# One-bank PSUM tiles for the layers that follow an attention, in place of its two-bank tiles

## The chip, the cores and the metric

One core of one Trainium2 chip. The metric is the device time of one execution in microseconds (us), as the median of several runs.

## The reference, cut to what matters

An attention with 16 heads (2 batches of 8, 768 positions, 64 wide), masked to keys of the query's hash bucket, feeds two dense layers over 1536 tokens of width 512:

```python
q_bits = (np.einsum('bhsd,dk->bhsk', q, proj) > 0)      # k_bits in the same way
mask = q_bucket[:, :, :, None] == k_bucket[:, :, None, :]
scores = np.where(mask, scale * np.matmul(q, k.transpose(0, 1, 3, 2)), -1000000000.0)
attn = softmax(scores); x = np.matmul(attn, v)          # to rows of 512
h = x @ w_in;  x = (h - np.tanh(h)) @ w_out             # first layer, 2048 wide
g = x @ w_gate; silu = g * (1.0 / (1.0 + np.exp(-g)))
return (silu * (x @ w_val)) @ w_out2                    # second layer, 1536 wide
```

## The kernel before, in words

**Order.** Nothing is looped on the chip. Every step is declared once to `Plan.op` (a step is a group of instructions on one engine) with the keys that it reads and writes, an estimated duration and a due time. `Plan.order` plays these through and gives one fixed order for all engines; the loops at the end of `lsh_attention_moe_kernel` write the instructions out in it. Keys name single PSUM banks: `("s", z, 0)`, `("s", z, 1)`, `("t", 0)`, `("t", 1)`, `("x", 0)`, `("h", 0)`. The waits on the chip are not written in the kernel: the framework puts them in, from what each instruction reads and writes of a tile.

**Attention.** A step of 128 queries makes its scores (L653) in one of two `s` tiles of two banks, one bank for each half of the 768 keys. VectorE takes the maximum over both banks (L662), ScalarE the exponentials (L664); TensorE transposes the result into the two banks of the one `t` tile (L682), and a copy empties it (L688). The product with the values goes to `x` (L706). All eight banks are taken: two `s` tiles of two banks, a `t` tile of two, `x` and `h` of one each.

**Layers.** The layers start while the attention ends. A unit is 256 columns of `w_in`, `w_gate` or `w_val` for one half of the tokens. By a scheme of the Strassen kind it takes seven products, each of six matmuls of 128x384 (L850). Products 0, 3, 5 and 6 add up in the first bank of one `s` tile, products 1 and 4 in the second bank of that tile, and product 2 takes a bank of a ring of four (`t` 0, `t` 1, `x`, `h`). Units take the two `s` tiles in turn. Between products ScalarE copies a bank out (`snap`, L830) and VectorE adds such a copy (`add`, L833). A finished block gets tanh (L791) or the sigmoid (L798), a subtraction or product on VectorE or GpSimd (L779), and is split in a high part (ScalarE, L784) and a low part (L779), into `op`. The block of product 4 stays in its bank for all of this. Here the steps read the second bank while products 5 and 6 write the first:

```python
PRODUCTS = (
    ("A11", "B11", 0, True), ("S1", "T1", 2, True), ("A12", "B21", 1, True), ("S2", "T2", 0, False),
    ("S4", "B22", 2, False), ("S3", "T3", 0, False), ("A22", "T4", 0, False),
)
banks = [s_t[z][:, 0, 0:TB], None, s_t[z][:, 1, 0:TB]]
RING = [(("t", 0), t_t[0][:, 0, :]), (("t", 1), t_t[0][:, 1, :]), (("x", 0), x_t[0]), (("h", 0), h_t[0])]
```

An output group is six matmuls (L904; 384 columns in layer 1, 512 in layer 2) into a bank of the same ring, emptied by L914, L915, L917, L928 or L933, and in part added up in memory by a DMA on GpSimd's queue (L941, L950). The order mixes products with output groups.

**Weights.** They come as 64-bit floats in 68 chunks, loaded into two `raw` buffers by SyncE (L271). VectorE makes each into 32-bit numbers (L273, L276, L279), then they are combined and split (L285, L287, L305, L307, L322, L324). A load waits until VectorE has done with the chunk two before it.

Of the kernel before, what the change touches and what calls it, by code (L numbers as in the profile page):

```python
# [21 lines left out]
TB = 384  # L22
NTK = NB * S
NSB = NTK // S
DM = 512
# [39 lines left out]
class Plan:  # L65
# [9 lines left out]
    def __init__(self):  # L75
        self.ops = []
        self.writers, self.readers = {}, {}
        self.n_first = 0

    def op(self, eng, fn, r=(), w=(), due=0.0, lat=None, late=False, after=0.0, alt=None, port=()):  # L80
        n = len(self.ops)
        deps = set()
        for k in r:
            deps.update(self.writers.get(k, ()))
        for k in w:
            deps.update(self.writers.get(k, ()))
            deps.update(self.readers.get(k, ()))
        for k in r:
            self.readers.setdefault(k, []).append(n)
        for k in w:  # L90
            if k in r:
                self.writers.setdefault(k, []).append(n)
            else:
                self.writers[k] = [n]
                self.readers[k] = []
        deps.discard(n)
        eng = {e: t * (1 if e == "PE" or not self.n_first else self.SAFE) for e, t in eng.items()}
        self.ops.append((eng, fn, deps, due, self.LAT if lat is None else lat, late, after,
                         DUE["alt"] if alt is None else alt, port))
# [86 lines left out]
def lsh_attention_moe_kernel(ctx: ExitStack, tc: tile.TileContext, qT, kT, vP, proj, cst, wts, out):  # L186
# [41 lines left out]
    ones_b = csb[:, 128:129]  # L228
    bias_b = csb[:, 129:130]
    pj = const.tile([128, 32], F32, name="pj")  # L230
    s_t = tiles(ctx, "s", 2, [128, 2, 512], space=PSUM)
    t_t = tiles(ctx, "t", 1, [128, 2, 512], space=PSUM)
    x_t = tiles(ctx, "x", 1, [128, 512], space=PSUM)
    h_t = tiles(ctx, "h", 1, [128, 512], space=PSUM)
    late = {}

    counts = {}

# [537 lines left out]
    EARLY, XDUE, EALT, ZDUE = 14, 13, 1.0, (-4, 4)  # L776

    def tt(dst, dk, a, ak, b, bk, alu, due, port):
        op({"DVE": dve(TB), "POOL": pool(TB)} if port else {"DVE": 0.56}, lambda e: e.tensor_tensor(out=dst, in0=a, in1=b, op=alu),  # L779
           r=[ak, bk], w=dk, due=due, alt=ALT, port=BOTH * port)  # L780

    def split_g(key, src, sk, due, psum):
        (hi, hk, h1), (lo, lk, l1) = g_slot(), g_slot()
        op({"ACT": 0.52}, lambda g: g.activation(out=hi, in_=src, func=ACTF.Copy), r=[sk], w=[hk] + h1, due=due)  # L784
        tt(lo, [lk] + l1, src, sk, hi.bitcast(F32), hk, ALU.subtract, due + 0.6, not psum)
        gh[key] = hi, lo, [hk, lk]


    def block_tanh(key, src, sk, due, psum, keep, spare=None):
        t, tk, t1 = spare or t_slot(1)  # L790
        op({"ACT": 0.51}, lambda e: e.activation(out=t, in_=src, func=ACTF.Tanh), r=[sk], w=[tk] + t1, due=due)  # L791
        d, dk = (src, sk) if keep else (t, tk)
        tt(d, [dk], src, sk, t, tk, ALU.subtract, due + 0.6, not psum)
        split_g(key, d, dk, due + 1.2, keep and psum)

    def block_silu(key, src, sk, due, psum, keep, spare=None):
        t, tk, t1 = t_slot(2)
        op({"ACT": 0.51}, lambda e: e.activation(out=t, in_=src, func=ACTF.Sigmoid), r=[sk], w=[tk] + t1, due=due)  # L798
        tt(t, [tk], src, sk, t, tk, ALU.mult, due + 0.6, not psum)
        sg[key] = t, tk  # L800

# [8 lines left out]
        ("S4", "B22", 2, False), ("S3", "T3", 0, False), ("A22", "T4", 0, False),  # L810
    )

    RING = [(("t", 0), t_t[0][:, 0, :]), (("t", 1), t_t[0][:, 1, :]), (("x", 0), x_t[0]), (("h", 0), h_t[0])]

    def bank_slot():
        return RING[ring("bank", len(RING))[1]]

    def products(name, i, sb):
        layer = 1 if name == "in" else 2
        after = due_at(nst - (EARLY if i < 2 else 14)) if layer == 1 else 0.0  # L820
        wk = need((name, i), clock[0], after)
        w = wi_t[wk[1]]
        z = sets[0] = 1 - sets[0]
        bkeys = [("s", z, 0), None, ("s", z, 1)]
        banks = [s_t[z][:, 0, 0:TB], None, s_t[z][:, 1, 0:TB]]
        (c0, k0, f0), (c1, k1, f1), (c2, k2, f2) = c_slot(), c_slot(), c_slot()
        block = {"in": block_tanh, "gate": block_silu, "val": block_val}[name]

        def snap(dst, dk, bank, bk, due):
            op({"ACT": 0.49}, lambda e: e.activation(out=dst, in_=bank, func=ACTF.Copy), r=[bk], w=dk, due=due)  # L830

        def add(dst, dk, bank, bk, c, ck, due):
            op({"DVE": 0.56}, lambda e: e.tensor_tensor(out=dst, in0=bank, in1=c, op=ALU.add), r=[bk, ck], w=[dk], due=due)  # L833

        def product(n):
            xn, wn, bi, first = PRODUCTS[n]
            if bi == 1:
                bkeys[1], b = bank_slot()
                banks[1] = b[:, 0:TB]
            bank, bk = banks[bi], bkeys[bi]  # L840
            d = clock[0]
            clock[0] += 6 * MM3
            wi = WN[wn]
            wp = wk + ("aaabbcc"[wi],)

            def mm(e):
                m = 0
                for k in range(2):
                    for wpart, xpart in terms:
                        e.matmul(  # L850
                            out=bank, lhsT=w[:, wpart, wi * 256 + k * 128:wi * 256 + k * 128 + 128],
                            rhs=x_at(sb, xn, xpart, k), start=first and m == 0, stop=m == 5, skip_group_check=True,
                        )
                        m += 1

            op({"PE": 6 * MM3}, mm, r=[wp + (0,), wp + (1,)] + [("X", sb, xn, h, k) for h in range(2) for k in range(2)]
               + [bk] * (not first), w=[bk], due=d, lat=0.25)
            e = clock[0]
            if n == 0:
                snap(c0, [k0] + f0, bank, bk, e)  # L860
            elif n == 1:
                snap(c1, [k1] + f1, bank, bk, e)
            elif n == 2:
                add(bank, bk, bank, bk, c0, k0, e)
                block((layer, i, sb, 0, 0), bank, bk, e + 0.6, True, True, (c0, k0, []))
            elif n == 3:
                snap(c2, [k2] + f2, bank, bk, e - 1)
            elif n == 4:
                add(bank, bk, bank, bk, c2, k2, e)
                block((layer, i, sb, 0, 1), bank, bk, e + 0.6, True, True, (c2, k2, []))  # L870
            elif n == 5:
                add(c1, k1, bank, bk, c1, k1, e - 1)
                block((layer, i, sb, 1, 1), c1, k1, e + 1, False, False)
            else:
                block((layer, i, sb, 1, 0), bank, bk, e, True, False)

        return product
# [4 lines left out]
    def out_group(layer, i, sb, j):  # L882
# [6 lines left out]
        t, m = divmod(j, n)  # L889
        size = (TB, DM)[layer - 1]  # L890
        gs = [gh[layer, i, sb, t, f] for f in range(2)]
        k, ps = bank_slot()
        ps = ps[:, 0:size]

        def mm(e):
            c = 0
            for f in range(2):
                w = wo_t[wks[f][1]]
                for wpart, gpart in terms:
                    if layer == 1:  # L900
                        lhs, rhs = w[:, wpart, m * 128:m * 128 + 128], gs[f][gpart]
                    else:
                        lhs, rhs = gs[f][gpart][:, m * 128:m * 128 + 128], w[:, wpart, :]
                    e.matmul(out=ps, lhsT=lhs, rhs=rhs, start=c == 0, stop=c == 5)  # L904
                    c += 1

        op({"PE": dur}, mm, r=[wk + (h,) for wk in wks for h in range(2)] + [g for gg in gs for g in gg[2]], w=[k],
# [3 lines left out]
        if layer == 1 and i in (0, NP1 - 1):  # L911
            if i == 0:
                op({"DVE": dve(TB), "ACT": 0.5}, lambda g:
                   g.activation(out=acc_at(sb, j), in_=ps, func=ACTF.Copy) if g is nc.scalar else  # L914
                   g.tensor_copy(acc_at(sb, j), ps), r=[k], w=[("acc", sb, j)], due=e, late=True)  # L915
            else:
                op({"DVE": 0.57}, lambda g: g.tensor_tensor(  # L917
                    out=acc_at(sb, j), in0=ps, in1=acc_at(sb, j), op=ALU.add,
                ), r=[k, ("acc", sb, j)], w=[("acc", sb, j)], due=e, late=True)
        elif layer == 2 and i == NP2 - 1:  # L920
            if m == 0:
# [3 lines left out]
                op({"SP": 0.5}, lambda g, at_=parts[0][0]: g.dma_start(out=at_(3).rearrange("p (j c) -> p j c", j=3), in_=o),  # L925
                   r=[("o", sb, t)], w=[key for _, key, _ in parts] + [k for _, _, f in parts for k in f], due=e - 25, lat=4.0)
            at_, key = stages["last"][m]
            op({"DVE": dve(DM)}, lambda g: g.tensor_tensor(out=at_(), in0=ps, in1=at_(), op=ALU.add), r=[k, key], w=[key], due=e)  # L928
            op({"SP": 0.5}, lambda g: g.dma_start(out=out[sb * S + j * 128:sb * S + j * 128 + 128, :], in_=at_()), r=[key], w=[], due=e)
        else:  # L930
            at_, key, first = stage(layer, m)
            op({"ACT": 0.18 + size / 1200, "DVE": dve(size)}, lambda g, at_=at_:
               g.activation(out=at_(), in_=ps, func=ACTF.Copy) if g is nc.scalar else g.tensor_copy(at_(), ps),  # L933
               r=[k], w=[key] + first, due=e, late=layer == 2, alt=EALT)
            if m == 0:
                stages[layer, "at"] = at_
# [74 lines left out]
        out_group(*outs.pop(0))  # L1011

    order, first_late = plan.order()
    with tc.manual_schedule():
        for n, e, _ in order[:first_late]:
            plan.ops[n][1](eng[e])
        at.close()
        with ExitStack() as mo:
            late["x1"] = tiles(mo, "x1", 1, [128, NG * TB], F32R)[0]
# [61 lines left out]
```

## Time and profile before

| | |
|---|---|
| median of 3 runs | 803.41 us (802.49 to 804.92) |
| the profiled execution | 803.86 us, span 802.1 us |
| TensorE matmuls, weight loads | 766.6 us, 661.5 us busy |
| VectorE, ScalarE, GpSimd | 589.4, 466.8, 359.7 us busy |
| granted clock of TensorE | 1.0 over the whole span |
| chain that ended last | TensorE 76%, VectorE 11%, DMA 4%, ScalarE 3% of the span |

PE is TensorE's matmuls and PEld its weight loads, DVE VectorE, ACT ScalarE, POOL GpSimd, SP SyncE. A group of instructions is named by line, engine, operation and tiles, as `PE L850 MATMUL s<-x,wi`: buffer numbers are left out, so that `s` is any bank of either `s` tile. Idle time is put down to what released the waiting instruction. Six matmuls of 384 columns start over 1.04 us when nothing waits, and a matmul's row reaches past its weight load's, so a short wait shows in the weight loads first.

### The profile page before, as it was taken

The numbers are of one execution on the slowest core, as the hardware profiler recorded it, in microseconds if no ns is written. First come the engines' busy times: TensorE is split into PE (matmuls) and PEld (weight loads), VectorE is DVE, ScalarE is ACT, GpSimd is POOL, SyncE is SP. The second block draws the span as 40 slices with busy tenths as digits, with TensorE's granted clock in tenths as the row PEclk, the third lists the DMA queues.
The fourth block names the chain that finished last, engine by engine and source line by source line (L and its number), as shares of the span: only waits on it lengthen the run. The fifth ranks groups of instructions, "written<-read, shape, count | busy, mean of one in ns | idle before, by whom it ended". The sixth has DMA issues, their size and how long they took to land.

```text
span 802.1 us, 12309 instructions
## 1 busy us (share of the span) xinstructions
PE 766.6 (96%) x4332; PEld 661.5 (82%) x4332; DVE 589.4 (73%) x1038; ACT 466.8 (58%) x906; POOL 359.7 (45%) x384
## 2 busy tenths in 40 slices
PE   5999999999999999999999999989989999999997
PEld 3766666666668889999999999989979898989996
DVE  6877777787698966786777668777765876877444
ACT  4787787786666754666545545554544455555530
POOL 4655567744475341343323454735245532344121
PEclk9999999999999999999999999999999999999999
DMA  7655444553222143777776761324327567666675
GB/s 213 161 131 139 109 133 115 124 134 74 73 66 93 53 117 94 165 189 177 178 171 161 157 142 47 86 79 158 120 73 149 128 150 158 121 155 132 119 167 187
DMA packets 38717, 104.23 MB, mean 130 GB/s; under 512 B 4704, under 2 KB 10080, under 8 KB 38656
## 3 DMA queue, kind: packets, MB, share of 16 engines
q1 hardware_dynamic: 28288, 71.06, 29.0%
q0 software_dynamic: 9904, 31.59, 22.9%
q10 hardware_dynamic: 464, 0.80, 0.4%
q8 instruction: 34, 0.56, 0.3%
q14 instruction: 27, 0.22, 0.1%
HBM read 49.17 MB, written 18.87 MB: 85 GB/s over the span
## 4 chain that ended last, share of the span: by engine, by line
PE 76%; DVE 11%; DMA 4%; ACT 3%; issue 3%; POOL 2%; SPq 0%; DVEq 0%; ACTq 0%; POOLq 0%
PE s L850 26%; PE t L904 13%; PE x L706 7%; PE t L682 7%; PE s L653 7%; PE h L904 6%; PE x L904 4%; DMA raw<-in_w 3%; DVE m L662 2%; PE x L850 2%; PE t L850 1%; ACT ct L664 1%; DMA acc<-ct 1%; DVE ct L779 1%; DVE op L779 1%
## 5 line engine op out<-in xcount | busy, mean ns | idle before, releaser
L850 PE MATMUL s<-x,wi 128*128 128x384 f32 x1200 | 235.1, 337 | 6.4 <-DVE ct L833 2.1
L850 PEld LDWEIGHTS s<-x,wi 128*128 128x128 f32 x1200 | 209.1, 188 | 18.6 <-DVE ct L833 4.0
L662 DVE TENSOR_REDUCE m<-s 128x1 f32<-128x768 f32 x96 | 89.3, 951 | 29.3 <-PE s L653 28.7
L671 POOL TENSOR_SCALAR ct<-ct,r 128x768 f32<-128x768 f32 x96 | 94.1, 988 | 33.4 <-DVE r L670 29.2
L664 ACT ACTIVATE ct<-s,m 128x768 f32<-128x768 f32 x96 | 85.8, 896 | 20.6 <-DVE m L662 19.7
L653 PE MATMUL s<-op 128*128 128x384 f32 x384 | 88.9, 366 | 6.7 <-ACT ct L664 6.4
L830 ACT ACTIVATE ct<-s 128x384 f32<-128x384 f32 x120 | 58.1, 490 | 58.6 <-PE s L850 58.1
L682 PEld LDWEIGHTS t<-csb,ct 128*128 128x128 f32 x576 | 64.4, 141 | 31.2 <-issue 18.7
L682 PE MATMUL t<-csb,ct 128*128 128x128 f32 x576 | 81.6, 278 | 5.2 <-POOL ct L671 1.7
L904 PE MATMUL t<-op,wo 128*128 128x384 f32 x384 | 77.0, 338 | 4.8 <-DVE acc L917 1.5
L653 PEld LDWEIGHTS s<-op 128*128 128x128 f32 x384 | 66.5, 195 | 17.5 <-ACT ct L664 15.3
L904 PEld LDWEIGHTS t<-op,wo 128*128 128x128 f32 x384 | 66.9, 188 | 7.8 <-DVE acc L917 2.1
L706 PE MATMUL x<-pt,v 128*64 128x384 f32 x384 | 69.0, 495 | 0.0
L287 POOL TENSOR_TENSOR wi<-fs,wi 128x512 fp32r<-128x512 f32 (+1 forms) x37 | 57.1, 1553 | 24.1 <-ACT wi L285 18.0
L904 PE MATMUL t<-wo,op 128*128 128x512 f32 x264 | 67.5, 393 | 0.0
L688 ACT ACTIVATE pt<-t 128x768 f32<-128x768 f32 x59 | 47.9, 811 | 29.7 <-PE t L682 28.6
L324 POOL TENSOR_TENSOR wo<-f,wo 128x512 fp32r<-128x512 f32 x17 | 22.4, 1316 | 75.1 <-ACT wo L322 70.9
L904 PEld LDWEIGHTS t<-wo,op 128*128 128x128 f32 x264 | 48.9, 188 | 8.2
L850 PE MATMUL s<-op,wi 128*128 128x384 f32 x240 | 48.2, 337 | 1.8 <-DVE ct L779 1.6
L706 PEld LDWEIGHTS x<-pt,v 128*64 128x64 f32 x384 | 24.7, 136 | 28.4 <-issue 28.4
L285 ACT ACTIVATE wi<-fs 128x512 fp32r<-128x512 f32 (+1 forms) x60 | 41.5, 701 | 10.4 <-DVE fs L305 4.0
L779 POOL TENSOR_TENSOR ct<-ct 128x384 f32<-128x384 f32 x20 | 20.6, 1029 | 59.9 <-ACT ct L791 31.0
(164 smaller groups left out, 1378.8 us busy)
## 6 DMA issues: line engine op xcount, KB each, us to landing
raw<-in_w SPq DMA_DIRECT2D x68, 512.0 KB, 3.9
acc<-ct POOLq DMA_DIRECT2D x24, 768.0 KB, 6.0
out<-acc POOLq DMA_DIRECT2D x16, 768.0 KB, 7.8
op<-raw SPq DMA_DIRECT2D x42, 192.0 KB, 3.0
op<-f SPq DMA_DIRECT2D x56, 96.0 KB, 2.5
v<-in_v SPq DMA_DIRECT2D x8, 384.0 KB, 3.2
out<-acc SPq DMA_DIRECT2D x4, 768.0 KB, 4.1
acc<-out SPq DMA_DIRECT2D x4, 768.0 KB, 4.5
```

Of the source, the lines that this page charges most:

```text
L285: op({"ACT": 0.19 + n / 1175}, lambda e: e.activation(out=hi, in_=src, func=ACTF.Copy), r=rk, w=[wk + (0,)], due=due, late=late)
L287: op({"POOL": pool(n), "DVE": dve(n)}, lambda e: e.tensor_tensor(out=lo, in0=src, in1=hi.bitcast(F32), op=ALU.subtract), r=rk + [wk + (0,) ...
L653: g.matmul(out=s[:, kh, 0:TB], lhsT=(b, a)[first][:, q0], rhs=ks[kh][0 if first else 1], start=first, stop=not first,)
L662: op({"DVE": 0.87}, lambda g: g.tensor_reduce(out=m, in_=sv, axis=AX.XY, op=ALU.max, negate=True), r=[sk + (0,), sk + (1,)], w=[mk], due=d ...
L664: op({"ACT": 0.9}, lambda g: g.activation(out=p.rearrange("p (a b) -> p a b", a=2), in_=sv, func=ACTF.Exp, bias=m, accum_out=sm), r=[sk + ...
L671: op({"POOL": 0.95}, lambda g: g.tensor_scalar(out=p, in0=p, scalar1=r, scalar2=1.0, op0=ALU.mult, op1=ALU.mult), r=[pk, rk], w=[pk], due= ...
L682: g.transpose(out=t_t[0][:, kt // 3, c0:c0 + 128], in_=p[:, kt * 128:(kt + 1) * 128], identity=ident)
L688: op({"ACT": 0.75, "DVE": 0.87}, lambda g: g.activation(out=dst, in_=src, func=ACTF.Copy) if g is nc.scalar else g.tensor_copy(dst, src), ...
L706: g.matmul(out=x[r, :], lhsT=v[:, kt, r], rhs=pt_t[ptks[e][1]][:, kt, :], start=(kt == 0), stop=(kt == NKT - 1), tile_position=(0, 64 * e),)
L830: op({"ACT": 0.49}, lambda e: e.activation(out=dst, in_=bank, func=ACTF.Copy), r=[bk], w=dk, due=due)
L850: e.matmul(out=bank, lhsT=w[:, wpart, wi * 256 + k * 128:wi * 256 + k * 128 + 128], rhs=x_at(sb, xn, xpart, k), start=first and m == 0, st ...
L904: e.matmul(out=ps, lhsT=lhs, rhs=rhs, start=c == 0, stop=c == 5)
```

## The change

The two `s` tiles and the `t` tile are now each in a pool with an exit stack of its own. The plan notes the `s` and `t` keys of every step. When the last attention step that touches one of these three tiles has been written out, `narrow` closes its pool and opens two pools of one bank each in its place. The layers' steps look their bank up by key at the time when they are written out (`bank_at`, `now`). Keys, durations and due times are the same, hence also the order of the instructions. The attention's own steps are not touched.

```diff
         deps.discard(n)
+        self.banks[n] = {("t", 0) if k[0] == "t" else k[:2] for k in (*r, *w) if k[0] in ("s", "t")}
...
-    s_t = tiles(ctx, "s", 2, [128, 2, 512], space=PSUM)
-    t_t = tiles(ctx, "t", 1, [128, 2, 512], space=PSUM)
     x_t = tiles(ctx, "x", 1, [128, 512], space=PSUM)
     h_t = tiles(ctx, "h", 1, [128, 512], space=PSUM)
-    late = {}
+
+    wide = {k: ExitStack() for k in (("t", 0), ("s", 0), ("s", 1))}
+    t_t = tiles(wide["t", 0], "t", 1, [128, 2, 512], space=PSUM)
+    s_t = [tiles(wide["s", z], "s%d" % z, 1, [128, 2, 512], space=PSUM, side=("left", "right")[z])[0] for z in range(2)]
+    late = {("x", 0): x_t[0], ("h", 0): h_t[0]}
...
-    RING = [(("t", 0), t_t[0][:, 0, :]), (("t", 1), t_t[0][:, 1, :]), (("x", 0), x_t[0]), (("h", 0), h_t[0])]
+    RING = [("t", 0), ("t", 1), ("x", 0), ("h", 0)]
...
+    def bank_at(key, size):
+
+        return lambda: late[key][:, 0:size]
+
+    def now(ap):
+        return ap() if callable(ap) else ap
+
+    def narrow(key):
+        wide[key].close()
+        keys = [("t", 0), ("t", 1)] if key[0] == "t" else [key + (0,), key + (1,)]
+        for k in keys:
+            late[k] = tiles(ctx, "b%s%d%d" % (*key, k[-1]), 1, [128, 512], space=PSUM, side="right")[0]
...
-        banks = [s_t[z][:, 0, 0:TB], None, s_t[z][:, 1, 0:TB]]
+        banks = [bank_at(bkeys[0], TB), None, bank_at(bkeys[2], TB)]
...
     order, first_late = plan.order()
+    last = {}
+    for i, (n, e, _) in enumerate(order):
+        for key in plan.banks.get(n, ()) if n < plan.n_first else ():
+            last[key] = i
+    ends = {i: key for key, i in last.items()}
     with tc.manual_schedule():
-        for n, e, _ in order[:first_late]:
+        for i, (n, e, _) in enumerate(order[:first_late]):
             plan.ops[n][1](eng[e])
+            if i in ends:
+                narrow(ends[i])
```

In all other steps of the layers a bank `ps`, `src` or `bank` becomes `ps()`, `now(src)` or `bank()`.

## Rows read from the trace of the kernel before

**Rows 1.** The page, busy time by engine (share of the span, instructions).

```profile
PE 766.6 (96%) x4332; PEld 661.5 (82%) x4332; DVE 589.4 (73%) x1038; ACT 466.8 (58%) x906; POOL 359.7 (45%) x384
```

**Rows 2.** Busy time by stretch: PE, PEld, DVE, ACT, POOL, granted clock, DMA share, GB/s.

```profile
246.00:490.00 244.00, 239.22 (x1351) 229.55 (x1350) 183.11 (x316) 137.46 (x286) 91.34 (x81) 1.00 0.57 139
...
535.00:612.00 77.00, 74.37 (x385) 67.71 (x384) 56.52 (x101) 38.13 (x75) 35.23 (x30) 1.00 0.42 127
612.00:780.00 168.00, 166.00 (x865) 153.04 (x863) 115.12 (x204) 84.49 (x164) 58.89 (x50) 1.00 0.66 140
```

**Rows 3.** Waits of the weight loads, 247 to 802 us: total us, times, longest.

```profile
PEld s L850 <- DVE ct L779: 4.5, 9, 1.0
PEld s L850 <- DVE ct L833: 4.0, 4, 1.9
PEld s L850 <- ACT ct L830: 3.4, 5, 1.1
PEld s L850 <- DVE op L779: 3.2, 3, 1.6
PEld t L904 <- DVE acc L917: 2.1, 2, 1.4
...
PEld s L850 <- ACT op L784: 1.9, 8, 0.2
PEld t L904 <- DVE op L779: 1.7, 2, 1.0
PEld t L904 <- ACT ct L791: 1.0, 1, 1.0
PEld t L904 <- ACT acc L914: 1.0, 1, 1.0
PEld s L850 <- DVE s L779: 0.9, 2, 0.5
PEld t L904 <- DVE t L779: 0.8, 1, 0.8
PEld t L850 <- issue: 0.6, 1, 0.6
PEld h L904 <- ACT ct L791: 0.6, 1, 0.6
PEld t L904 <- ACT op L784: 0.6, 1, 0.6
PEld t L904 <- DVE ct L933: 0.5, 1, 0.5
```

**Rows 4.** Groups of weight loads, 247 to 802 us: busy, mean ns, idle before.

```profile
L904 PEld LDWEIGHTS t<-op,wo 128*128 128x128 f32 x384 | 66.9, 188 | 7.8 <-DVE acc L917 2.1 <-DVE op L779 1.7 <-ACT ct L791 1.0
...
L904 PEld LDWEIGHTS x<-op,wo 128*128 128x128 f32 x198 | 34.8, 188 | 0.0
```

**Rows 5.** Timeline, 416 to 419 us: start, length, instruction, idle before.

```profile
416.18 0.49 ACT L830 ACTIVATE ct<-s 128x384 f32<-128x384 f32 x1 [0.93 <-PE s L850]
...
416.56 0.49 ACT L784 ACTIVATE op<-s 128x384 fp32r<-128x384 f32 x1
417.11 1.00 PEld L850 LDWEIGHTS s<-x,wi 128*128 128x128 f32 x6 [0.24 <-ACT op L784]
...
418.53 0.56 DVE L779 TENSOR_TENSOR op<-s,op 128x384 fp32r<-128x384 f32 x1 [1.31 <-PE s L850]
```

**Rows 6.** Timeline, 510 to 516 us.

```profile
510.81 1.01 POOL L779 TENSOR_TENSOR op<-ct,op 128x384 fp32r<-128x384 f32 x1
...
515.33 1.00 PEld L904 LDWEIGHTS t<-op,wo 128*128 128x128 f32 x6 [1.43 <-DVE acc L917]
```

**Rows 7.** Timeline, 582 to 584 us.

```profile
582.66 0.56 DVE L779 TENSOR_TENSOR ct<-s,ct 128x384 f32<-128x384 f32 x1 [2.29 <-PE s L850]
...
583.27 0.99 PEld L850 LDWEIGHTS s<-op,wi 128*128 128x128 f32 x6 [1.04 <-DVE ct L779]
```

**Rows 8.** Waits of VectorE, 247 to 802 us: total us, times, longest.

```profile
DVE fs L273 <- DMA raw<-in_w: 9.5, 4, 3.6
```

More of the change, by code (lines that the diff above doesn't have):

```diff
@@ L78, in __init__ @@
         self.n_first = 0
+        self.banks = {}
     def op(self, eng, fn, r=(), w=(), due=0.0, lat=None, late=False, after=0.0, alt=None, port=()):
@@ L778, in tt @@
     def tt(dst, dk, a, ak, b, bk, alu, due, port):
-        op({"DVE": dve(TB), "POOL": pool(TB)} if port else {"DVE": 0.56}, lambda e: e.tensor_tensor(out=dst, in0=a, in1=b, op=alu),
+        op({"DVE": dve(TB), "POOL": pool(TB)} if port else {"DVE": 0.56}, lambda e: e.tensor_tensor(out=now(dst), in0=now(a), in1=b, op=alu),
            r=[ak, bk], w=dk, due=due, alt=ALT, port=BOTH * port)
@@ L783, in split_g @@
         (hi, hk, h1), (lo, lk, l1) = g_slot(), g_slot()
-        op({"ACT": 0.52}, lambda g: g.activation(out=hi, in_=src, func=ACTF.Copy), r=[sk], w=[hk] + h1, due=due)
+        op({"ACT": 0.52}, lambda g: g.activation(out=hi, in_=now(src), func=ACTF.Copy), r=[sk], w=[hk] + h1, due=due)
         tt(lo, [lk] + l1, src, sk, hi.bitcast(F32), hk, ALU.subtract, due + 0.6, not psum)
@@ L790, in block_tanh @@
         t, tk, t1 = spare or t_slot(1)
-        op({"ACT": 0.51}, lambda e: e.activation(out=t, in_=src, func=ACTF.Tanh), r=[sk], w=[tk] + t1, due=due)
+        op({"ACT": 0.51}, lambda e: e.activation(out=t, in_=now(src), func=ACTF.Tanh), r=[sk], w=[tk] + t1, due=due)
         d, dk = (src, sk) if keep else (t, tk)
@@ L797, in block_silu @@
         t, tk, t1 = t_slot(2)
-        op({"ACT": 0.51}, lambda e: e.activation(out=t, in_=src, func=ACTF.Sigmoid), r=[sk], w=[tk] + t1, due=due)
+        op({"ACT": 0.51}, lambda e: e.activation(out=t, in_=now(src), func=ACTF.Sigmoid), r=[sk], w=[tk] + t1, due=due)
         tt(t, [tk], src, sk, t, tk, ALU.mult, due + 0.6, not psum)
@@ L829, in snap @@
         def snap(dst, dk, bank, bk, due):
-            op({"ACT": 0.49}, lambda e: e.activation(out=dst, in_=bank, func=ACTF.Copy), r=[bk], w=dk, due=due)
+            op({"ACT": 0.49}, lambda e: e.activation(out=dst, in_=bank(), func=ACTF.Copy), r=[bk], w=dk, due=due)
         def add(dst, dk, bank, bk, c, ck, due):
-            op({"DVE": 0.56}, lambda e: e.tensor_tensor(out=dst, in0=bank, in1=c, op=ALU.add), r=[bk, ck], w=[dk], due=due)
+            op({"DVE": 0.56}, lambda e: e.tensor_tensor(out=now(dst), in0=bank(), in1=c, op=ALU.add), r=[bk, ck], w=[dk], due=due)
         def product(n):
@@ L837, in product @@
             if bi == 1:
-                bkeys[1], b = bank_slot()
-                banks[1] = b[:, 0:TB]
+                bkeys[1] = bank_slot()
+                banks[1] = bank_at(bkeys[1], TB)
             bank, bk = banks[bi], bkeys[bi]
@@ L850, in mm @@
                         e.matmul(
-                            out=bank, lhsT=w[:, wpart, wi * 256 + k * 128:wi * 256 + k * 128 + 128],
+                            out=bank(), lhsT=w[:, wpart, wi * 256 + k * 128:wi * 256 + k * 128 + 128],
                             rhs=x_at(sb, xn, xpart, k), start=first and m == 0, stop=m == 5, skip_group_check=True,
@@ L891, in out_group @@
         gs = [gh[layer, i, sb, t, f] for f in range(2)]
-        k, ps = bank_slot()
-        ps = ps[:, 0:size]
+        k = bank_slot()
+        ps = bank_at(k, size)
         def mm(e):
@@ L903, in mm @@
                         lhs, rhs = gs[f][gpart][:, m * 128:m * 128 + 128], w[:, wpart, :]
-                    e.matmul(out=ps, lhsT=lhs, rhs=rhs, start=c == 0, stop=c == 5)
+                    e.matmul(out=ps(), lhsT=lhs, rhs=rhs, start=c == 0, stop=c == 5)
                     c += 1
@@ L913, in out_group @@
                 op({"DVE": dve(TB), "ACT": 0.5}, lambda g:
-                   g.activation(out=acc_at(sb, j), in_=ps, func=ACTF.Copy) if g is nc.scalar else
-                   g.tensor_copy(acc_at(sb, j), ps), r=[k], w=[("acc", sb, j)], due=e, late=True)
+                   g.activation(out=acc_at(sb, j), in_=ps(), func=ACTF.Copy) if g is nc.scalar else
+                   g.tensor_copy(acc_at(sb, j), ps()), r=[k], w=[("acc", sb, j)], due=e, late=True)
             else:
                 op({"DVE": 0.57}, lambda g: g.tensor_tensor(
-                    out=acc_at(sb, j), in0=ps, in1=acc_at(sb, j), op=ALU.add,
+                    out=acc_at(sb, j), in0=ps(), in1=acc_at(sb, j), op=ALU.add,
                 ), r=[k, ("acc", sb, j)], w=[("acc", sb, j)], due=e, late=True)
@@ L927, in out_group @@
             at_, key = stages["last"][m]
-            op({"DVE": dve(DM)}, lambda g: g.tensor_tensor(out=at_(), in0=ps, in1=at_(), op=ALU.add), r=[k, key], w=[key], due=e)
+            op({"DVE": dve(DM)}, lambda g: g.tensor_tensor(out=at_(), in0=ps(), in1=at_(), op=ALU.add), r=[k, key], w=[key], due=e)
             op({"SP": 0.5}, lambda g: g.dma_start(out=out[sb * S + j * 128:sb * S + j * 128 + 128, :], in_=at_()), r=[key], w=[], due=e)
@@ L932, in out_group @@
             op({"ACT": 0.18 + size / 1200, "DVE": dve(size)}, lambda g, at_=at_:
-               g.activation(out=at_(), in_=ps, func=ACTF.Copy) if g is nc.scalar else g.tensor_copy(at_(), ps),
+               g.activation(out=at_(), in_=ps(), func=ACTF.Copy) if g is nc.scalar else g.tensor_copy(at_(), ps()),
                r=[k], w=[key] + first, due=e, late=layer == 2, alt=EALT)
```

## The prediction

> **What bounds the kernel now.** I read the busy time first: TensorE's matmuls are busy for 766.6 us of 802.1 and no other engine comes near [rows 1]. The stretches then say where TensorE loses time: the attention (to about 246 us) is not touched, and from there to 780 us matmuls fill all but a few us of each stretch, at a granted clock of 1.00 (the 2.4 GHz level), with VectorE at 115 of 168 us at most and ScalarE and GpSimd below it [rows 2]. So the layers go at TensorE's pace, and only its waits can be won. They are small and many. The matmul rows hide part of them, since a matmul's row reaches past its weight load, so I take them from the weight loads: the fifteen groups add up to 26.8 us [rows 3]. That is the most that any change to waits alone could give.
>
> **Whose waits these are.** The names already say something: the output groups take `t` 0, `t` 1, `x` and `h` in turn, yet the 384 loads into `t` lost 7.8 us and the 198 into `x` none [rows 4]; `h` lost 0.6 once [rows 3]. The two tiles in which waits gather are the two that hold two banks. The timeline shows one case in full. At 417.11 product 5 of a unit begins to write the first bank of its `s` tile. What it needs there, the `snap` of that bank, ended at 416.18 + 0.49 = 416.67. It starts 0.05 us after the high part of product 4's block ended (416.56 + 0.49 = 417.05), and that reads the *second* bank. The mirror image follows: the low part of that block, ready at 417.05, starts at 418.53, after 1.31 us of wait for product 5's matmuls, which write the other bank [rows 5]. So a wait holds between any two accesses of which one writes, as soon as they share the tile, bank or no bank.
>
> The Trainium skill (PSUM — Partial Sum Buffer, section "PSUM bank collisions raise a hardware error") asks for a guard by bank and quadrant and not by address. If the guards of before stood by bank, the change would remove nothing and the time would stay at 803.4 us; the 0.24 and 1.31 us of [rows 5] speak against that, and by them the guard is wider than the rule asks.
>
> **The change, part by part.**
>
> *Waits of TensorE across the halves of a tile go.* The order is fixed, so for each wait of [rows 3] I set two ends side by side: the last instruction that the plan's keys name for that group, and the last one on the sibling bank. Where the sibling's is later, the start follows it by about 0.05 us each time; what is won is the wait down to the end of the named one, if that comes later than TensorE itself. By row of [rows 3]: all 1.9 of ACT op L784 (eight copies of the case above), all 2.1 of acc L917, 2.5 of the 3.4 of ACT ct L830, 2.2 of the 3.2 of s <- DVE op L779, 1.6 of the 4.5 of DVE ct L779, 0.9 of s L779, 0.8 of t L779, 1.0 of ct L791 into t, 0.5 of the 1.0 of acc L914, 0.6 of t <- ACT op L784, 0.5 of ct L933. Sum 14.6 us. The largest is at 515.33: an output group into one half of `t` waits 1.43 us for L917 reading the other half, while its operand was ready at 510.81 + 1.01 = 511.82 [rows 6]. The other 26.8 - 14.6 = 12.2 us are waits on the bank's own readers or on operands, and stay unless their releaser comes earlier.
>
> *Waits of VectorE and ScalarE across halves go.* Most of these engines' idle time costs nothing. In two places it was passed on to TensorE. At 582.66 VectorE starts a step that had waited 2.29 us for matmuls into the other half, and TensorE's wait of 1.04 us at 583.27 ends with it [rows 7]. At 285.65 the 1.0 us wait of t <- DVE op L779 [rows 3] has the same cause one half of `t` over. Together 2.1 us.
>
> *What is late next.* TensorE's own loop (product, block, output group) moves forward as a whole, and so do the buffers that it frees. A weight load does not: it is issued when VectorE has done with the chunk two before, and takes its time. Four times VectorE already stood for a load, 9.5 us in all [rows 8]; on TensorE three of the four waits for ct L833 follow such a load, 3.3 of that row's 4.0 us [rows 3]. When VectorE loses its waits, it comes to further loads sooner, and some that just arrive in time now will be late. Bounds: nothing (most of the idle time that VectorE sheds lies before work on blocks, not before a load), or 7.8 us (the rival below). I take 3.3, as much again as the three cost now: an estimate, nearer to that row than to the rival.
>
> *The handover.* Closing a pool writes no instruction by the diff. The first layer matmuls on each new bank wait for all that touched the old tile, which they did before: the first on `t` lost 0.6 us [rows 3]. Price between nothing and three times that, 1.8 us; I take nothing, for the last reader of each wide tile is in any case the step after which it is closed, a reader of both banks. The other edits (the lookup by key, the note of keys) happen while the program is written and cost nothing on the chip. Neither the number of matmuls, copies and DMAs nor their queues change, so no queue is passed by anything. Bank numbers do change; no row shows a bank's number to matter, since groups with the same shape take 188 ns a weight load in `t` and in `x` [rows 4].
>
> *Sum.* Against the profiled execution: 803.86 - 14.6 - 2.1 + 3.3 = 790.5 us. That execution lies 0.45 above the median of the runs, so 790.0 us for the median.
>
> **The rivals.**
>
> *The loads take over (about 795 us).* Suppose that, with VectorE's waits gone, the loads pace the middle of layer 1 (335 to 466 us) and the first third of layer 2 (535 to 612 us). What TensorE saves there is then given back: of the waits above, by their starts, 3.6 us in the first, 3.2 and the 1.0 of 583.27 in the second, 7.8 in all. Then 803.4 - 16.7 + 7.8 = 794.5, or some us more where the three late loads after 612 us grow too. For it: [rows 8], and DMAs busy for 0.57 and 0.42 of these stretches [rows 2]. Against it: TensorE, at 74.37 of 77 us in the second, is still the fuller one, and a late load has reached it only in part (9.5 us at VectorE became 3.3). The Trainium skill (TensorE: Matmul & The Clock Gate, section "HAM oscillation — how this bites in real kernels") tells of a kernel where more PSUM buffers brought nothing beside load waits; no row here shows such a case.
>
> *The change does not do what it says (803.4 us).* If the waits came from how the framework counts an engine's finished work and not from the tile, one-bank tiles would keep them. For it: a wait names an engine's latest step, and rows are inferred. Against it: `x` and `h` are served by the same engines in the same order and show almost none [rows 3, 4].
>
> *Slower: loads and accumulating DMAs fall on each other (about 811 us).* TensorE, no longer held, would bring the output groups' DMAs to where the weight loads of layer 2 stand. A late load costs TensorE 3.3 / 3 = 1.1 us. Layer 2 has 36 chunks, three late now. If 25 were late, 22 x 1.1 = 24 us come on against 16.7 won: 803.4 + 7.5 = 811. It decides from 15 further late loads on. For it: the DMAs are busiest in just that stretch, 0.66 [rows 2]. Against it: loads and output groups follow the same fixed order and both move forward, so their places to each other hardly change.
>
> **How the numbers follow.** Forecast (waits go, a little comes back): 0.76. Loads take over: 0.15. No effect: 0.05. Slower: 0.04. The measurement can tell some 0.3% (2.4 us) from no change; the first two are clearly beyond it, so faster 0.91, same 0.05, slower 0.04. Range: at the low end nothing comes back and a third of the remaining 10.1 us (12.2 less the 2.1) goes too, because ScalarE and VectorE answer sooner [rows 5]: 803.4 - 16.7 - 3.4 = 783.3. At the high end the loads take over, the handover costs its 1.8 and the late loads grow by a little: 797. The range of 783.5 to 797 leaves out the last two cases and the edges of the first two.
>
> **What would show it right or wrong.** Instruction counts and each engine's order are the same, and the attention's part ends at the same time. The weight loads' waits of the layers fall from 26.8 to about 13 us: the eight waits for ACT op L784 and the two for acc L917 are gone, and with product 5 no step of product 4's block waits any more. Matmul rows into the former `t` banks lose no more than those into `x`. VectorE's 9.5 us for loads stay or grow to some 13. I am wrong if waits across sibling banks remain, if the load waits grow by more than 8 us and come back in TensorE's rows, or if new waits stand at the three handovers.

## The result, and the profile after

The change takes the median from 803.9 us to 784.63 us (783.77 to 785.25, 4 runs): 19.3 us less, a ratio of 0.9761 (95% interval 0.9742 to 0.978). The forecast was 790.0 in a range of 783.5 to 797: right in sign and cause, 5.4 us short in size.

The page after, busy time by engine:

```profile
PE 756.1 (97%) x4332; PEld 662.3 (85%) x4332; DVE 589.2 (75%) x1038; ACT 469.2 (60%) x906; POOL 359.7 (46%) x384
```

The instructions of each engine are as many as in [rows 1]. Busy times differ by at most 2.4 us (ScalarE), except for the matmuls, which are busy for 10.5 us less. A group that has waited has a longer row: in the timeline of before, the six matmuls at 515.33, whose loads stand in [rows 6], take 1.31 us where 1.20 is usual, and so do those at 417.11 and 583.27. So the busy time of before held a part of the waits.

The longest stretch after, columns as in [rows 2]:

```profile
246.00:490.00 244.00, 243.81 (x1409) 240.30 (x1408) 193.28 (x330) 144.80 (x298) 96.39 (x84) 1.00 0.57 139
```

In it 1408 weight loads fit where 1350 did. Lines have moved by 4 to 17: L867 is the products' line (L850 before), L921 the output groups' (L904), L783 and L788 the old L779 and L784, L847 and L850 the old L830 and L833, L934 and L950 the old L917 and L933, L277 the old L273; `bs` and `bt` are the new one-bank tiles. All waits of the weight loads after, 247 to 802 us, as in [rows 3] (the attention's x L710 apart):

```profile
PEld bs L867 <- DVE ct L850: 3.6, 3, 1.6
...
PEld bs L867 <- DVE ct L783: 1.4, 2, 1.0
PEld bt L867 <- issue: 0.6, 1, 0.6
PEld h L921 <- issue: 0.6, 1, 0.6
PEld x L921 <- DVE op L783: 0.5, 1, 0.5
```

That is 6.7 us of the 26.8: 20.1 us of waits are gone, about 1 us more than the span lost (802.1 - 783.1 = 19.0). A sixteenth row of before, a wait of 0.4 us for `x` from L363 on VectorE, is not in the 26.8; it is gone too. The two halves of a former pair are called siblings from here on; no wait for a sibling bank is among the rest. Layer 1's loads for output groups in the former `t` banks now lose nothing, where the row below stood at 7.8 in [rows 4]; those into `x`, which had lost nothing, wait 0.5 us once, for an operand:

```profile
L921 PEld LDWEIGHTS bt<-op,wo 128*128 128x128 f32 x384 | 67.4, 188 | 0.0
```

And the case of [rows 5], in the timeline after:

```profile
409.64 0.49 ACT L788 ACTIVATE op<-bs 128x384 fp32r<-128x384 f32 x1
409.92 1.05 PEld L867 LDWEIGHTS bs<-x,wi 128*128 128x128 f32 x6
...
410.21 0.55 DVE L783 TENSOR_TENSOR op<-bs,op 128x384 fp32r<-128x384 f32 x1
```

Product 5's loads start at 409.92, right behind the loads before them, while ScalarE reads the other half until 410.13; the low part on VectorE starts at 410.21, 0.08 us after its input, where it had waited 1.31 us for the matmuls.

### The profile page after: what moved, and what is told of

Same layout as the page of the kernel before. It is cut to its first block, busy times and chain, and to the rows that moved or that the text cites. A ratio compares the mean times of both kernels' runs of the same rounds, so it can differ in the third digit from the quotient of the medians.

```text
span 783.1 us, 12290 instructions
## 1 busy us (share of the span) xinstructions
PE 756.1 (97%) x4332; PEld 662.3 (85%) x4332; DVE 589.2 (75%) x1038; ACT 469.2 (60%) x906; POOL 359.7 (46%) x384
## 4 chain that ended last, share of the span: by engine, by line
PE 83%; DVE 6%; DMA 6%; issue 2%; ACT 2%; POOL 1%; SPq 0%; ACTq 0%; POOLq 0%; DVEq 0%
PE bs L867 29%; PE bt L921 15%; PE t L686 7%; PE x L710 7%; PE h L921 7%; PE s L657 7%; PE x L921 5%; DMA raw<-in_w 4%; PE x L867 2%; DVE m L666 2%; PE bt L867 2%; DMA fs<-in_qT 1%; PE h L867 1%; ACT ct L668 1%; DVE pt L692 1%
## 5 line engine op out<-in xcount | busy, mean ns | idle before, releaser
L867 PE MATMUL bs<-x,wi 128*128 128x384 f32 x1200 | 231.9, 335 | 2.3 <-DVE ct L850 2.3
L867 PEld LDWEIGHTS bs<-x,wi 128*128 128x128 f32 x1200 | 210.6, 188 | 8.3 <-DVE ct L850 3.6
L847 ACT ACTIVATE ct<-bs 128x384 f32<-128x384 f32 x120 | 58.8, 490 | 54.9 <-PE bs L867 54.3
L921 PE MATMUL bt<-op,wo 128*128 128x384 f32 x384 | 75.6, 334 | 0.0
L710 PE MATMUL x<-pt,v 128*64 128x384 f32 x384 | 69.0, 495 | 0.0
L921 PE MATMUL bt<-wo,op 128*128 128x512 f32 x264 | 67.6, 393 | 0.0
L921 PEld LDWEIGHTS bt<-op,wo 128*128 128x128 f32 x384 | 67.4, 188 | 0.0
L291 POOL TENSOR_TENSOR wi<-fs,wi 128x512 fp32r<-128x512 f32 (+1 forms) x37 | 55.1, 1508 | 23.0 <-ACT wi L289 16.9
L921 PEld LDWEIGHTS bt<-wo,op 128*128 128x128 f32 x264 | 49.0, 188 | 8.1
L710 PEld LDWEIGHTS x<-pt,v 128*64 128x64 f32 x384 | 24.7, 136 | 28.4 <-issue 28.4
L867 PE MATMUL bs<-op,wi 128*128 128x384 f32 x240 | 47.5, 335 | 0.6 <-DVE ct L783 0.6
L783 POOL TENSOR_TENSOR ct<-ct 128x384 f32<-128x384 f32 x20 | 21.0, 1048 | 54.6 <-ACT ct L795 27.4
```

Source lines behind the costliest of these rows:

```text
L291: op({"POOL": pool(n), "DVE": dve(n)}, lambda e: e.tensor_tensor(out=lo, in0=src, in1=hi.bitcast(F32), op=ALU.subtract), r=rk + [wk + (0,) ...
L710: g.matmul(out=x[r, :], lhsT=v[:, kt, r], rhs=pt_t[ptks[e][1]][:, kt, :], start=(kt == 0), stop=(kt == NKT - 1), tile_position=(0, 64 * e),)
L847: op({"ACT": 0.49}, lambda e: e.activation(out=dst, in_=bank(), func=ACTF.Copy), r=[bk], w=dk, due=due)
L867: e.matmul(out=bank(), lhsT=w[:, wpart, wi * 256 + k * 128:wi * 256 + k * 128 + 128], rhs=x_at(sb, xn, xpart, k), start=first and m == 0, ...
L921: e.matmul(out=ps(), lhsT=lhs, rhs=rhs, start=c == 0, stop=c == 5)
```

## The experiments

All are made from the kernel after. Ratios are to the kernel before, timed on the same chip. Differences to the kernel after are to its 784.63 us, which come from another comparison; timed again it gave 785.91 us, so such a difference holds to about 1.5 us. Where a kernel has lines added, the lines behind them stand up to 6 further down: L867 is L871 in the runs that reopen pairs, L869 in those with added waits and L873 in the one with three banks.

**The handover alone.** The tiles are closed and reopened, but as pairs.

```diff
         keys = [("t", 0), ("t", 1)] if key[0] == "t" else [key + (0,), key + (1,)]
+        if True:
+            pair = tiles(ctx, "b%s%d" % key, 1, [128, 2, 512], space=PSUM, side="right")[0]
+            late.update({k: pair[:, i, :] for i, k in enumerate(keys)})
+            return
```

> The three tiles are closed and reopened at the same places as after, but each again as one tile of two banks. Theory (the time was lost to waits between the two banks of a shared tile): all of these waits are back, 803.9 us within 1.5, weight loads of the layers wait about 26 us. Rival (closing the pools, or the other bank numbers, brought the gain): 785 to 795 us.

Measured 804.24 us, ratio 1.0004 (0.9993 to 1.0014). TensorE's waits are back row by row, 26.3 us in all; three of them:

```profile
PEld bs L871 <- DVE ct L783: 4.4, 9, 1.0
...
PEld bt L925 <- DVE acc L938: 2.1, 2, 1.4
...
PEld bs L871 <- ACT op L788: 1.9, 8, 0.2
```

Closing and opening pools costs nothing that can be measured, and other places for the tiles bring nothing. It is the tile of two banks.

**TensorE's waits alone, the readers' waits alone, both.** One-bank tiles stay; explicit dependencies on the sibling bank's last accesses are added, for groups on TensorE in one kernel, for the steps on ScalarE and VectorE in the other, for all in the third. `seen` holds, for each bank and engine, the last step that read it and the last that wrote it. The added part is the same in all three but for the condition on the engine `e`, here `e == "PE"`:

```diff
...
+            sib = k[:-1] + (1 - k[-1],)
+            for oe, (reads, writes) in seen.get(sib, {}).items():
+                for was in (writes, reads if k in wk else None):
+                    if was is not None and oe != e and e == "PE":
+                        tc.add_manual_dep(new[0], was, mybir.DependencyInfo(
+                            mybir.DependencyClass.Sync, mybir.DependencyReason.ANTI), reason="pair")
...
```

> One-bank tiles as after, but TensorE's groups get back the waits for ScalarE's and VectorE's accesses to the sibling bank; those engines don't get theirs for TensorE and each other. Theory by the prediction's sum: TensorE's own cross-bank waits are 14.6 of the 19.3 us, so about 799 us. Rival (the readers' waits for TensorE started the delays, and TensorE's came from them): under 790 us, since without late readers the sibling bank is free in time.

Measured 791.67 us, 0.9851 (0.9837 to 0.9866): 7.0 us over the kernel after, half of what the prediction's sum gives TensorE's own waits, and between the two expectations. TensorE's waits are 13.9 us in all, 7.2 more than after the change. The eight waits of 0.24 us for the high part come back in full, the large ones only in part; for acc the row was 2.1 in two waits [rows 3]:

```profile
PEld bs L869 <- ACT op L790: 1.9, 8, 0.2
...
PEld bt L923 <- DVE acc L936: 1.2, 1, 1.2
```

> The mirror: ScalarE and VectorE get back their waits across sibling banks, TensorE does not. Theory by the prediction's sum: 2.1 us were passed on to TensorE, and what the sum missed (19.3 - 13.4, about 5) may lie here too: 787 to 790 us. Rival (readers' waits are the root): 795 us or more.

Measured 791.37 us, 0.9845 (0.9829 to 0.9861): 6.7 us, between the two expectations. TensorE has no wait of its own for a sibling bank here, yet its waits rise from 6.7 to 13.0 us, as results that it needs come late. The three largest rows (after the change the first stood at 3.6, the second at 1.4, the third did not exist), and a row of VectorE's waits that has come back:

```profile
PEld bs L869 <- DVE ct L852: 5.1, 5, 1.6
PEld bs L869 <- DVE ct L785: 2.9, 5, 1.0
PEld bt L923 <- DVE op L785: 2.0, 3, 1.0
```

```profile
DVE op L785 <- PE bs L869: 13.8, 13, 1.5
```

> One-bank tiles as after, with both sets of cross-bank waits put back, those of TensorE and those of its readers. Each set alone cost 7.0 and 6.7 us. If they only add: 798.3 us. Theory (they feed each other: a reader held by TensorE is the reader that TensorE then waits for): the missing 5 us come back as well, 802 to 804.5 us, and the rows of weight load waits are those of the kernel before.

Measured 803.4 us, 0.9994 (0.9984 to 1.0003). So the two sets make up the whole effect, and 19.3 - 7.0 - 6.7 = 5.6 us of it exist only with both. Against the second timing of the kernel after (785.91) the two sets cost 5.8 and 5.5 us alone and the rest is larger still, so this part is not noise. TensorE's waits say the same: 26.3 us here, 19.6 more than after, of which the two sets alone bring 7.2 and 6.3. The order is the same in all these kernels, so their groups can be matched one by one; seven waits of this run, 4.6 us, stand in neither of the other two. One of them:

```profile
594.54 0.49 ACT L849 ACTIVATE ct<-bs 128x384 f32<-128x384 f32 x1 [2.67 <-PE bs L869]
...
595.44 0.56 DVE L785 TENSOR_TENSOR op<-bs,op 128x384 fp32r<-128x384 f32 x1 [1.80 <-ACT op L790]
...
596.05 0.30 PEld L869 LDWEIGHTS bs<-x,wi 128*128 128x128 f32 x2 [0.60 <-DVE op L785]
```

ScalarE's copy starts only when TensorE's products are through, the low part on VectorE comes later with it, and TensorE's next product waits 0.60 us for that low part. With TensorE's waits alone the copy starts while the products still run, and the same low part ends 0.53 us before the same loads start (584.46 and 584.99 in that run). With the readers' waits alone the low part is held, but TensorE does not wait for it (583.07 and 583.12). So a reader held by TensorE's matmuls into the sibling bank is itself the reader that TensorE's next group then waits for; the other six were not followed like this.

**One kind of tile alone.** The same edit as for the handover, for `s` only and for `t` only.

```diff
+        if key[0] == "s":
+            pair = tiles(ctx, "b%s%d" % key, 1, [128, 2, 512], space=PSUM, side="right")[0]
+            late.update({k: pair[:, i, :] for i, k in enumerate(keys)})
+            return
```

> Only the t tile gives way to one-bank tiles, the s tiles are reopened with two banks. Theory: the waits of output groups into t go, 5.5 us by their rows and 1.0 passed on by VectorE: 803.9 - 6.5 = 797.4 us. Rival (the s tiles' waits set the pace of the loop and swallow it): above 801 us.

Measured 795.79 us, 0.9898 (0.9884 to 0.9913): 8.1 us gained, 1.6 more than its rows. The rival falls.

> The mirror of the run with t alone: only the two s tiles give way to one-bank tiles, t is reopened with two banks. Theory by the rows of before: 9.1 us of waits into s and 1.0 passed on, 803.9 - 10.1 = 793.8. If the two parts simply add, the run with t alone (8.1 us gained of 19.3) leaves 11.2 for s: 792.7. Rival (each part gains only once the other is gone): above 797 us.

Measured 795.47 us, 0.9896 (0.9881 to 0.9911), 7.8 us under the kernel before beside it: between the theories and the rival. By its rows `s` is the larger part, yet it gains no more than `t`. With `t` still shared, `t` waits in one place where it had not; the row below has no counterpart in [rows 3]:

```profile
PEld bt L925 <- ACT ct L851: 1.7, 1, 1.7
```

Together 8.1 + 7.8 = 15.9 of 19.3 us. Whether the 3.4 us left come only with both is not settled: each of the three numbers holds to 1 to 1.5 us, and TensorE's waits fall by 8.7 and 10.9 us, which together is nearly the whole.

**The cost enlarged.** `s` has one-bank tiles; `t` and `h` share one tile of three banks.

```diff
-    h_t = tiles(ctx, "h", 1, [128, 512], space=PSUM)
+    h_s = ExitStack()
+    h_t = tiles(h_s, "h", 1, [128, 512], space=PSUM)
...
+        if key[0] == "t":
+            h_s.close()
+            three = tiles(ctx, "bt", 1, [128, 3, 512], space=PSUM, side="right")[0]
+            late.update({k: three[:, i, :] for i, k in enumerate(keys + [("h", 0)])})
+            return
```

> The suspected cost is enlarged: s has one-bank tiles, and both t banks and h share one tile of three banks, so that of the ring of four three share (three pairs of siblings in place of the one of the kernel before); x stays alone. Theory (sharing a tile is the cause, for any bank): h, whose loads lost almost nothing before, now waits like t, and the t part of the loss, some 8 us with one pair, becomes 16 to 24: 800 to 809 us. Rival (something particular to the t banks): as with t alone wide, 792 to 794 us.

Measured 822.4 us, 1.0231 (1.0213 to 1.0248): 37.8 us over the kernel after, more than the theory gave, and the rival falls. Layer 1's weight loads for output groups into that tile (`bt` now counts `h`'s too), and into `x`:

```profile
L927 PEld LDWEIGHTS bt<-op,wo 128*128 128x128 f32 x570 | 98.4, 188 | 28.2 <-DVE bt L784 10.0 <-ACT op L789 4.1 <-ACT ct L956 3.3
...
L927 PEld LDWEIGHTS x<-op,wo 128*128 128x128 f32 x198 | 34.7, 188 | 0.6 <-DVE op L784 0.6
```

The first lost 28.2 us, `x`, still alone, 0.6. Matched group by group with the kernel before, whose order is the same, the output groups of both layers wait 8.1 us for `h`, where it was 0.6, and 25.3 us for `t`, where it was 7.6 (idle time that has no releaser is not counted). So `h` pays as soon as it shares a tile. The price grows somewhat faster than the pairs: the run with `s` alone narrowed has one pair, in `t`, and lies 10.8 us over the kernel after, with 9.6 us more waits of TensorE; three pairs cost 37.8 us and 38.6 us of waits. A likely reason, not tested by itself: the ring's order is `t` 0, `t` 1, `x`, `h`, so with `h` in the tile two of the four steps around the ring go to a sibling, where it was one.

**What late loads still cost.** The loads of layer 2 are left out; the conversions stay.

```diff
-        op({"SP": 0.5}, lambda e: e.dma_start(out=raw, in_=wts[c]),
+        op({"SP": 0.5}, lambda e: e.dma_start(out=raw, in_=wts[c]) if c < 32 else None,
```

> The kernel after without the loads of the 36 weight chunks of layer 2: the conversions work on what the raw buffers held, and layer 2's result has no meaning. Measures what late loads still cost. Theory (the three waits for ct L850, 3.6 us, are the loads): these waits and VectorE's 11.8 us for loads go, 784.6 - 3.6 = 781 us. Rival (VectorE's order alone makes them late): 784 us or more.

Measured 781.72 us, 0.9727 (0.9713 to 0.9742): 2.9 us under the kernel after. The three waits for ct L850 are gone, and of VectorE's waits for loads this is left:

```profile
DVE fs L277 <- DMA raw<-in_w: 1.1, 1, 1.1
```

So the waits for ct L850 are late loads, and all loads of layer 2 together cost about 3 us in the kernel after.

**Loads planned as slow as they are.** One constant of the planner; the order of the instructions changes.

```diff
-           w=first([rk]), due=due - 8, lat=3.5, after=after)
+           w=first([rk]), due=due - 8, lat=3.5 if c < 32 else 7.0, after=after)
```

> The kernel after, with the planner told that a load of layer 2 takes 7.0 us instead of 3.5, as the late ones do: VectorE's order then puts other steps before a conversion. Theory (late loads stop VectorE's queue): part of the 3.6 us comes back, 781 to 784 us. Rival (a new order costs elsewhere what it saves): 784.6 us or more.

Measured 783.64 us, 0.9753 (0.9738 to 0.9768). A gain of 1 us over the kernel after is within what two separate comparisons can show, so both were run again side by side:

> The kernel after unchanged, beside the one with the planner's longer load time: 784.6 us within 1.

> The planner's longer load time again, beside the unchanged kernel after: if the gain is real it is 1 us, 783.6; if it was spread between runs, within 0.3 us of the kernel after.

785.91 us, 0.978 (0.9767 to 0.9792), 1.3 us over its first time, against 783.98 us, 0.9756 (0.9742 to 0.977). The two pairs say 1 and 2 us, the intervals just overlap: probably faster than the kernel after, not settled. Where it would come from shows in VectorE's waits for loads, in the kernel after and with the longer time:

```profile
DVE fs L277 <- DMA raw<-in_w: 11.8, 6, 3.3
```

```profile
DVE fs L277 <- DMA raw<-in_w: 1.8, 2, 1.0
```

The three waits of TensorE behind them go too; new rows of 0.5 to 1.1 us, for other steps of VectorE, take part of it back.

## Why the prediction was right, and where it was short

*What bounds the kernel, and whose waits these are:* right. TensorE's waits account for the gain to within 1 to 2 us, and the pairs of banks were the cause (handover alone: no change; both sets of waits put back: 803.4). The guard by bank and quadrant that the Trainium skill asks for (PSUM — Partial Sum Buffer, section "PSUM bank collisions raise a hardware error") was not what stood in the kernel before; its guards went by the tile, and those of the kernel after, with one bank to a tile, go by bank. One reading was off: of the stretches shown, VectorE's fullest is not 115 of 168 us but 183.11 of 244 [rows 2], 75% busy, which is still far from TensorE.

*Waits of TensorE across halves go, 14.6 us:* no wait for a sibling bank is left, so the term stands as a count of what vanished. As a cause it was too large: put back alone they cost 7.0 us. The rows of before show each wait as it was with the readers already late, and the sum took those ends as given.

*Waits of VectorE and ScalarE go, 2.1 us:* this is the term that was mis-sized. The prediction took two places where a held reader was passed on, and left the other 10.1 us of waits standing. The two places are right: both waits, 1.04 us each, come back with the readers' waits alone. But of the 12.2 us on the bank's own readers and on operands, 12.2 - 6.7 = 5.5 us went. The readers' waits alone cost 6.7 us when put back, and 5.6 more together with TensorE's. A sign was in VectorE's waits before, between 247 and 802 us:

```profile
DVE op L779 <- PE s L850: 16.1, 14, 1.7
```

By the prediction most of such idle time costs nothing. With the readers' waits put back this row returns (13.8 us), and TensorE then waits 2.0 us for low parts as operands, of which the prediction had counted 1.0; with both sets it also waits for them as readers of a sibling bank, as in the case at 596.05. How much of the 6.7 us comes from this row alone no run separates.

*What is late next, 3.3 us given back:* next to nothing was. VectorE's waits for loads grew from 9.5 [rows 8] to 11.8 us, within the 13 that were said, but TensorE felt 3.6 us of them where it had felt 3.3, in front of the same three groups. The 0.3 us more is already in the 6.7, so with the term above at 5.5 and none of its own for the loads the sum reads 803.86 - 14.6 - 5.5 = 783.8, against 784.94 for the profiled execution after. The two misses, 3.4 us on the readers and 3.3 on the loads, go the same way; together they are about 1 us more than the forecast was off by, which the rows do not explain. By the same two misses the weight loads' waits fell to 6.7 us and not to about 13.

*The handover, nothing:* right to about 1 us, by the run that has it alone; the first loads into the former `t` still wait 0.6 us. *The attention untouched:* its last exponentials start at 241.7 us where it was 242.1, its last product with the values, between the first groups of the layers, at 262.6 where it was 263.3.

*The rivals.* The loads do not take over: TensorE waits for late loads in front of the same three groups as before and nowhere else, and without the loads of layer 2 the kernel after is only about 3 us faster. No effect and slower are both excluded by the time. What the range's low end was built on, that nothing comes back and that ScalarE and VectorE answer sooner, is what happened, at 5.5 - 2.1 = 3.4 us. That this is just the third that it allowed for is luck: the third was a guess, and no row gave it.

## What to carry to other kernels

Give each PSUM bank that is used by itself a tile of its own. In this kernel a tile of several banks made writes to one bank wait for reads of the others, and the readers for the writes, and nothing in the code says so. Such waits show as releasers that work on the other half of the tile, spread over many places at a quarter of a us to two; sum them by releaser before deciding that a stage is full. When both sides of such a pair wait for each other, count the waits of the engine that is not the bottleneck too: those that lead to a buffer or an operand which the bottleneck wants next can lie on the path, however idle that engine is.

## What the runs showed that was not expected

Two kinds of waits that cost 7.0 and 6.7 us alone cost 19.3 us together, and three banks in one shared tile cost 37.8 us over none shared. With separate banks TensorE goes through 244 us with 243.81 us of matmul rows at a granted clock of 1.00, while VectorE, ScalarE and GpSimd read and write other banks and buffers all the time: no row showed a price for working in the neighbouring bank at the same moment.
